# Attention and expert routing on one core: query transposes in a bank of their own, expert tiles transposed by TensorE, the last expert's weights loaded later

## The chip, the cores and the metric

The kernel runs on one core of one Trainium2 chip, as a single launch. The metric is the device time of one execution in microseconds. Three runs of the kernel before gave 455.08, 456.19 and 462.63 us.

## What is computed

An attention whose queries are averaged in pairs, and behind it a mixture of experts in which each token goes to one expert given with the input. Cut to what matters:

```python
# q, k, v: (8 batches, 8 heads, 1152, 64)
q_pool = q.reshape(B, H, S // 2, 2, D).mean(axis=3)          # 576 queries
scores = (1 / sqrt(D)) * q_pool @ k.transpose(0, 1, 3, 2)    # 576 x 1152
attn = exp(scores - max);  attn = attn / sum(attn)
x = (attn @ v) as (8 * 576 = 4608 tokens, 512)
for e in range(8):                                           # w1: 512 x 1024, w2: 1024 x 512
    mask = domain_id == e
    out[mask] = relu(x[mask] @ w1[e]) @ w2[e]
```

## The kernel before

**Attention.** Two heads of a batch make a pair; there are 32 pairs. The pooled queries and the keys of a pair are laid side by side (head, depth), so that the 128 partitions hold 64 depths of one head and 64 of the other. A pair has 12 steps (`SPP`), 384 in all. A step is `score` (L593, PE: scores of both heads, 432 columns each, into a tile `s` of two PSUM banks, three of which rotate), `expo` (L605, ACT: one `exp` over 128 x 864) and, some steps later, `av` (L614, PE: 15 small matmuls a call into the bank `acc`). `evac` (L626, L628, DVE) divides by the sums, `put_x` (L643) writes finished tokens to the DRAM tensor `x_tok`, from SyncE's queue.

**Transposing keys and queries.** `prep_q` (L531) adds the two queries of a pair of rows, `prep_k` (L546) copies keys. `turn(p)` (L565) transposes both on PE, in halves of 64 rows, as 2 x (9 + 6) = 30 transposes, into one of the three `s` tiles; DVE then takes the keys out as `kq` (L570) and the queries as `qz` in two strided copies (L575). It stands at the fifth step of each pair.

**Expert tiles inside attention.** A token list is built early (the `rt_*` and `id_*` functions). From step 112 on, `get_x` (L653, GpSimd) gathers 128 tokens of one expert as a tile `xs`. Each fill tile is then transposed, multiplied by w1 (`up`, L802, 32 matmuls) and by w2 (`down`, L815, 8 matmuls) in the one PSUM bank `px` (pool `xps`, one buffer), and scattered to the output (L515). Three of the tiles are transposed on PE (`turn_x`, L770), the others by a DMA transpose from SyncE's queue (`flip_x`, L668). A planner sets how much fill stands between the attention steps: it walks the steps, gives each kind of work a cost in ns (`C_T` a turn, 222 a fill piece) and issues pieces as long as the debt stays under `LAG`. The order that it writes is the order on each engine; a manual schedule keeps it.

```python
STEP, C_MODE, C_S, C_T, C_AV, LAG = 771, 200, 190, 440, 150, 250
...
            if debt + work_ns + c_ - span > LAG:
                break
            fb.piece()
```

No new tile begins in the last pair. What a begun tile still lacks at the end of attention is issued there in one go.

**Expert runs behind attention.** `runs` lists what is left: first expert 5 (tiles 0 to 2), then the rest of experts 0 to 4, then expert 5's last two tiles, then experts 6 and 7 whole (5 tiles each). A run k is `stage1` (L1042, 32 matmul groups) and `stage2` (L1075, 8 matmuls a tile). The tiles of run 1 and of runs with 5 tiles are transposed by PE (`turn_tile`, L1060); those of the short runs 2 to 6 by DMA (`flip_x`), which SyncE issues while run k - 1 goes on. Weights of experts 0 to 5 are loaded inside attention; those of 6 and 7 (`load_w`, L496 to L505, four parts of 512 KB each from GpSimd's queue) are put in a list `wq` behind a run, and each following run issues two parts from it:

```python
        if i1 == NTC and rest:
            er = rest.pop(0)
            fns, wts[er] = load_w(er)
            wq.extend(fns)
```

So 6 follows run 1 and 7 follows run 2; 7's parts are issued in runs 4 and 5.

Of the kernel before, what the change touches and what calls it, by code (L numbers as in the profile page):

```python
# [9 lines left out]
P = 128  # L10
# [9 lines left out]
def kernel(  # L20
# [537 lines left out]
    def turn(p):  # L558
        kp, qp = kpt[p], qpt[p]
        new_kq(p)  # L560
        mt = spsum.tile([P, 2, 512], FP32, name="s")[:, :, :].bitcast(F16)
        for c in range(NC + NJ):
            src = kp[:, c, :, :] if c < NC else qp[:, c - NC, :, :]
            for r, (lo, hi) in enumerate(HALF):
                nc.tensor.transpose(  # L565
                    mt[:, r, c * 64 : c * 64 + 64],
                    in_=src[lo:hi, :, :].rearrange("p h d -> p (h d)"),
                    identity=ident16[lo:hi, lo:hi],
                )
        nc.vector.tensor_copy(  # L570
            kq[p][:, :].rearrange("p (c r k) -> p r c k", c=NC, r=2),
            mt[:, :, 0 : NC * 64].rearrange("p r (c k) -> p r c k", c=NC),
        )
        for r, n in ((0, 64), (1, QP - 64)):
            nc.vector.tensor_copy(  # L575
                qz[p % 2][:, :].rearrange("p (j k) -> p j k", j=NJ)[:, :, 64 * r : 64 * r + n],
                mt[:, r, NC * 64 : (NC + NJ) * 64].rearrange("p (j k) -> p j k", j=NJ)[:, :, 0:n],
            )


# [107 lines left out]
    }  # L688
    STEP, C_MODE, C_S, C_T, C_AV, LAG = 771, 200, 190, 440, 150, 250
    FILL, HELD = 5, len(WSTEP)  # L690
# [70 lines left out]

    tiles, turned, begun, turns = [], [], [], []

# [11 lines left out]

    BY_PE = [(0, 0), (0, 1), (0, 2)]

    def add_tile(e, i):
        h0 = {"xs": (e, i)}
        tiles.append((e, i))  # L780

        def turn_pe():
            h0["xt"] = fill.tile([P, ND, P], F16, name="xt0")
            turn_x(h0["xt"][:, :, :], e, i)
            begun.append((e, i))

        def turn_in():
            h0["xt"] = fill.tile([P, ND, P], F16, name="xt0")
            flip_x(h0["xt"][:, :, :], e, i)
            h0["t"] = now[0]  # L790

        def up(f):
            if f == 0:
                h0["h"] = fill.tile([P, NF, P], F16, name="h0")
                if (e, i) not in BY_PE:
                    begun.append((e, i))
                    turned.append((e, i))
            if f % 4 == 0:
                h0["m"] = spare([P, 4, P])
            m = h0["m"]  # L800
            for cc in range(ND):
                nc.tensor.matmul(  # L802
                    m[:, f % 4, :], lhsT=wts[e][0][:, cc, f * P : (f + 1) * P],
                    rhs=h0["xt"][:, cc, :], start=cc == 0, stop=cc == ND - 1,
                )
            if f % 4 == 3:
                nc.vector.tensor_scalar(  # L807
                    out=h0["h"][:, f - 3 : f + 1, :], in0=m[:, :, :],
                    scalar1=0.0, scalar2=None, op0=ALU.max,
                )  # L810
# [15 lines left out]

        if (e, i) in BY_PE:
            fb.blocks.append(([turn_pe], 230, 1, False, h0))
        else:
            turns.append((e, i, turn_in, len(tiles) - 1))  # L830
        for fn, lo, hi in ((up, 0, 4), (up, 4, NF), (down, 0, NF)):
            fb.blocks.append(([lambda f=f, fn=fn: fn(f) for f in range(lo, hi)], 222, 1, (e, i) in BY_PE or lo > 0 or fn is down, h0))

# [58 lines left out]

    debt = 0
    for t in range(NST + 4):
# [12 lines left out]
        elif main and s_ in (2, 6) and p + 3 < NPAIR:  # L907
            (load_k if s_ == 2 else load_v)(p + 3)
        work_ns, span = 0, 0
        for it in windows.get(t, ()):  # L910
            if it < 0:
                turn(-it)
                work_ns += C_T
            else:
                score(it)
                expo(it)
                work_ns += C_S
                span += STEP
# [30 lines left out]

        if turns and t >= got.get(turns[0][:2], NST) + 10 and turns[0][3] <= len(begun):  # L950
            turns.pop(0)[2]()
        if first and t >= got.get(first[0], NST) + 8:
# [3 lines left out]
        while t == NST - SPP and fb.cur is not None:  # L956
            fb.piece()
        while main and span:
            if fb.cur is None:
                if not fb.blocks or t < fb.ready or t >= NST - SPP:  # L960
                    break
                b_ = fb.blocks[0]
                x_ = b_[4]["xs"]
                at = got.get(x_, NST) if x_ in BY_PE else b_[4].get("t", NST)
                if not b_[3] and t < max(at + 11, WSTEP[x_[0]][3] + 14):
                    break
                c_ = b_[1]
            else:
                c_ = fb.cur[1]
# [125 lines left out]
    for k_, r in enumerate(runs):  # L1095
# [22 lines left out]
        for fn in last:  # L1118
            fn()
        if i1 == NTC and rest:  # L1120
            er = rest.pop(0)
            fns, wts[er] = load_w(er)
            wq.extend(fns)
# [65 lines left out]
```

## Time and profile before

| | |
|---|---|
| median of 3 runs (lowest, highest) | 456.19 us (455.08, 462.63) |
| the profiled execution: its time, its span | 459.37 us, 457.1 us |
| instructions | 14379 |
| busy in the span: PE, PE weight load | 400.5 us (88%), 254.5 us (56%) |
| ACT, DVE, GpSimd | 339.4 us (74%), 222.4 us (49%), 182.2 us (40%) |
| mean of the granted TensorE clock | 0.958 |

The span is the time between the first and the last profiled instruction; the profiled execution's own time has 2.3 us outside of it. It is 3.2 us above the median. The shares are means over two stages with different limits: attention with fill (to about 333 us), and the expert runs (from there on).

### The profile page before, as it was taken

Reading aid. Unit: us, or ns where it says so; the run is one execution under the profiler, and the core shown is the slowest. Engines: PE = TensorE matmul, PEld = TensorE weight load, DVE = VectorE, ACT = ScalarE, POOL = GpSimd, SP = SyncE. Lnnn points to the kernel's source line nnn. Section 1 sums busy time; section 2 is a strip of 40 time slices with the busy share of each in tenths; the row PEclk is TensorE's granted clock in tenths of the full one; section 3 lists DMA queues with packets and bytes.
Section 4 is the critical chain, followed back from the end, with each engine's and each line's share of the span. In section 5 each row is a group of like instructions: output and inputs, shape, how many; then the busy total and the mean of one; then the engine's idle time right before and its main releaser. Section 6 shows DMA issues by size and latency. Waiting matters only on the chain.

```text
span 457.1 us, 14379 instructions
## 1 busy us (share of the span) xinstructions
PE 400.5 (88%) x6193; PEld 254.5 (56%) x6193; DVE 222.4 (49%) x612; ACT 339.4 (74%) x447; POOL 182.2 (40%) x304
## 2 busy tenths in 40 slices
PE   7888888888999987999999999989888989699993
PEld 4455555655666555566666665665545544365551
DVE  4388698864565443556655455634222322133230
ACT  5889999999999996999999999979822212133221
POOL 5433223307264240622642345534136686221413
PEclk9589999999999998999999999989889999799998
DMA  8999999976999999689999969956624499941203
GB/s 204 239 229 194 234 248 180 183 171 129 203 216 259 233 172 203 131 158 204 194 214 242 205 123 213 216 124 130 128 58 137 134 195 220 208 104 40 94 8 111
DMA packets 60107, 78.70 MB, mean 172 GB/s; under 512 B 19695, under 2 KB 48784, under 8 KB 60034
## 3 DMA queue, kind: packets, MB, share of 16 engines
q0 software_dynamic: 38384, 66.93, 72.6%
q1 hardware_dynamic: 21378, 10.63, 12.2%
q8 instruction: 50, 0.82, 0.7%
q14 instruction: 23, 0.19, 0.1%
q10 hardware_dynamic: 272, 0.13, 0.1%
HBM read 95.46 MB, written 15.21 MB: 242 GB/s over the span
## 4 chain that ended last, share of the span: by engine, by line
ACT 34%; PE 28%; issue 15%; DMA 8%; POOL 7%; DVE 4%; SPq 1%; POOLq 1%; another core or an unknown queue 1%; DVEq 0%; ACTq 0%
ACT e L605 34%; PE acc L614 9%; PE s L593 8%; PE px L802 4%; POOL out_dram L515 4%; DMA xt<-xs 3%; PE px L815 3%; POOL xs L653 2%; DMA w2h<-in_moe_w_dram 2%; DVE xb L628 2%; PE hp L1042 1%; PE s L565 1%; DMA q<-in_q_dram 1%; DMA x_tok<-xb 1%; SPq L643 1%
## 5 line engine op out<-in xcount | busy, mean ns | idle before, releaser
L605 ACT ACTIVATE e<-s 128x864 f16<-128x864 f32 x384 | 306.7, 948 | 18.0 <-PE s L593 16.5
L593 PE MATMUL s<-qz,kq 64*128 64x432 f16 (+2 forms) x1152 | 123.0, 294 | 24.1 <-ACT e L605 20.0
L614 PEld LDWEIGHTS <-e 128*128 128x128 f16 x2880 | 103.3, 99 | 47.2 <-issue 23.6
L614 PE MATMUL acc<-v,e 128*128 128x65 f16 x2835 | 122.8, 196 | 6.5 <-DVE xb L628 5.5
L653 POOL DMA_INDIRECT xs<-x_tok,grow x40 | 41.6, 1041 | 105.9 <-DVE xs L93 55.9
L593 PEld LDWEIGHTS <-kq 64*128 64x128 f16 x1152 | 46.8, 95 | 63.3 <-issue 46.2
L515 POOL DMA_INDIRECT out_dram<-osb,gid x40 | 40.9, 1022 | 76.2 <-ACT osb L1081 20.7
L1042 PE MATMUL hp<-xt,w1h 128*128 128x256 f16 (+3 forms) x320 | 45.9, 303 | 7.3 <-DMA xt<-xs 5.7
L1075 PE MATMUL op<-w2h,hT 128*128 128x512 f16 x216 | 49.5, 379 | 2.3 <-DVE hT L1049 1.3
L1047 ACT ACTIVATE hT<-hp 128x256 f16<-128x256 f32 (+2 forms) x36 | 17.7, 490 | 43.8 <-PE hp L1042 33.0
L114 POOL DMA_DIRECT2D vs<-in_v_dram x32 | 24.0, 749 | 60.3 <-DVE v L540 43.9
L1042 PEld LDWEIGHTS <-w1h 128*128 128x128 f16 x352 | 32.7, 100 | 26.8 <-issue 10.2
L1049 DVE TENSOR_SCALAR hT<-hp 128x256 f16<-128x256 f32 (+2 forms) x36 | 20.1, 558 | 51.4 <-PE hp L1042 35.3
L626 DVE RECIPROCAL rr<-acc 128x5 f32<-128x5 f32 x63 | 12.3, 195 | 66.0 <-PE acc L614 58.7
L1081 ACT COPY osb<-op 128x512 f32<-128x512 f32 x16 | 9.4, 585 | 42.3 <-PE op L1075 36.8
L570 DVE COPY kq<-s 128x1152 f16<-128x1152 f16 x31 | 23.4, 755 | 30.2 <-PE s L565 23.1
L802 PE MATMUL px<-xt,w1h 128*128 128x128 f16 x416 | 33.4, 224 | 4.2 <-DMA xt<-xs 2.9
L1075 PEld LDWEIGHTS <-hT 128*128 128x128 f16 x216 | 20.6, 98 | 25.7 <-DVE hT L1049 2.1
L628 DVE TENSOR_TENSOR xb<-acc,rr 128x320 f16<-128x320 f32 x63 | 31.0, 492 | 3.2 <-DMA x_tok<-xb 1.0
L815 PE MATMUL px<-w2h,h 128*128 128x512 f16 x104 | 31.6, 399 | 0.8 <-DVE h L807 0.8
L531 DVE TENSOR_TENSOR qp<-q 96x768 f16<-96x768 f32 x31 | 29.4, 947 | 2.3 <-DMA q<-in_q_dram 2.3
L802 PEld LDWEIGHTS <-w1h 128*128 128x128 f16 x416 | 24.7, 100 | 9.0 <-issue 7.5
(134 smaller groups left out, 301.3 us busy)
## 6 DMA issues: line engine op xcount, KB each, us to landing
q<-in_q_dram POOLq DMA_DIRECT2D x28, 576.0 KB
vs<-in_v_dram POOLq DMA_DIRECT2D x32, 288.0 KB
k<-in_k_dram POOLq DMA_DIRECT2D x31, 288.0 KB
w1h<-in_moe_w_dram POOLq DMA_DIRECT2D x16, 512.0 KB
w2h<-in_moe_w_dram POOLq DMA_DIRECT2D x16, 512.0 KB
x_tok<-xb SPq DMA_DIRECT2D x22, 96.0 KB
q<-in_q_dram SPq DMA_DIRECT2D x3, 576.0 KB
x_tok<-xb SPq DMA_DIRECT2D x22, 64.0 KB
```

Source lines behind the costliest of these rows:

```text
L114: nc.gpsimd.dma_start(vs[:, :, :, :], v[b, h : h + 2].rearrange("h (p c) d -> p h c d", p=P))
L515: ins = nc.gpsimd.indirect_dma_start(out=dst[:, :], out_offset=bass.IndirectOffsetOnAxis(ap=ap, axis=0), in_=src, in_offset=None, **kw,)
L531: nc.vector.tensor_tensor(out=qp[0:QP, :, :, :].rearrange("p j h d -> p h j d"), in0=q2[:, :, :, 0:D], in1=q2[:, :, :, D : 2 * D], op=ALU.add,
L593: nc.tensor.matmul(s[:, r, o : o + n], lhsT=kq[p][lo:hi, c * P : (c + 1) * P], rhs=qz[p % 2][lo:hi, q0 : q0 + n], start=True, stop=True,)
L605: nc.scalar.activation(e_[:, :, o : o + W], st.pop(t)[:, :, 0:W], AF.Exp, bias=0.0, scale=0.0625)
L614: nc.tensor.matmul(acc[p, h][:, i * (D + 1) : (i + 1) * (D + 1)], lhsT=et[p, c // 3][:, h, o : o + P], rhs=v16[p % NV][:, c, h, 0 : D + 1] ...
L628: nc.vector.tensor_tensor(out=xb[b][:, :, o : o + D], in0=a[:, :, 0:D], in1=rr[:, :].unsqueeze(2).broadcast_to([P, NQ, D]), op=ALU.mult,)
L653: nc.gpsimd.indirect_dma_start(out=dst, out_offset=None, in_=x_dram[0 : 1 + nb * Sp, :], in_offset=bass.IndirectOffsetOnAxis(ap=ap, axis=0),)
L802: nc.tensor.matmul(m[:, f % 4, :], lhsT=wts[e][0][:, cc, f * P : (f + 1) * P], rhs=h0["xt"][:, cc, :], start=cc == 0, stop=cc == ND - 1,)
L815: nc.tensor.matmul(h0["o"][:, :], lhsT=h0["h"][:, f, :], rhs=wts[e][1][:, f, :], start=f == 0, stop=f == NF - 1,)
L1042: nc.tensor.matmul(hp_[:, lo : lo + n], lhsT=w1h[:, cc, f * P : (f + 1) * P], rhs=xt[:, cc, lo : lo + n], start=cc == 0, stop=cc == ND - 1,)
L1075: nc.tensor.matmul(op_[:, :], lhsT=hT[:, f, i * P : (i + 1) * P], rhs=w2h[:, f, :], start=f == 0, stop=f == NF - 1,)
```

## The change

Four things change, all in the order and the place of work; what is computed stays.

1. `turn` transposes the keys alone. The queries of a pair get a function of their own, `turn_q`: 6 transposes over full 96 rows into the bank `px`, and one copy of 128 x 576 by DVE. It is issued one to five steps into the pair before, in a window in which no fill tile is open (pairs 0 and 1: at steps 10 and 7).
2. All fill tiles are transposed by PE (`turn_x`), 10 steps after their gather at the earliest. The list of DMA transposes in attention is gone. Those for expert 5's first run (`xf`) and those of the runs stay.
3. The planner's cost of a turn is 270 in place of 440, and a `turn_q` costs 300.
4. The weights of expert 7 are put in the list behind run 4 in place of run 2.

By the planner 11 fill tiles stand in attention where 13 stood: expert 0 has three, experts 1 to 4 have two each (before: three each for 0 to 2, two for 3 and 4). The runs 2 and 3 have three tiles each in place of two.

```diff
     def turn(p):
-        kp, qp = kpt[p], qpt[p]
+        kp = kpt[p]
         new_kq(p)
         mt = spsum.tile([P, 2, 512], FP32, name="s")[:, :, :].bitcast(F16)
-        for c in range(NC + NJ):
-            src = kp[:, c, :, :] if c < NC else qp[:, c - NC, :, :]
+        for c in range(NC):
             for r, (lo, hi) in enumerate(HALF):
                 nc.tensor.transpose(
                     mt[:, r, c * 64 : c * 64 + 64],
-                    in_=src[lo:hi, :, :].rearrange("p h d -> p (h d)"),
+                    in_=kp[lo:hi, c, :, :].rearrange("p h d -> p (h d)"),
                     identity=ident16[lo:hi, lo:hi],
                 )
...
-        for r, n in ((0, 64), (1, QP - 64)):
-            nc.vector.tensor_copy(
-                qz[p % 2][:, :].rearrange("p (j k) -> p j k", j=NJ)[:, :, 64 * r : 64 * r + n],
-                mt[:, r, NC * 64 : (NC + NJ) * 64].rearrange("p (j k) -> p j k", j=NJ)[:, :, 0:n],
-            )
+
+    def turn_q(p):
+        qt = xps.tile([P, Sp], F16, name="px")
+        for j in range(NJ):
+            nc.tensor.transpose(
+                qt[:, j * QP : (j + 1) * QP],
+                in_=qpt[p][0:QP, j, :, :].rearrange("p h d -> p (h d)"),
+                identity=ident16[0:QP, 0:QP],
+            )
+        nc.vector.tensor_copy(qz[p % 2][:, :], qt[:, :])
...
-    STEP, C_MODE, C_S, C_T, C_AV, LAG = 771, 200, 190, 440, 150, 250
+    STEP, C_MODE, C_S, C_T, C_AV, LAG = 771, 200, 190, 270, 150, 250
...
-        if (e, i) in BY_PE:
-            fb.blocks.append(([turn_pe], 230, 1, False, h0))
-        else:
-            turns.append((e, i, turn_in, len(tiles) - 1))
+        fb.blocks.append(([turn_pe], 230, 1, False, h0))
...
+        if span and p + 1 < NPAIR and s_ >= qat and qdone == p:
+            while s_ > 7 and fb.cur is not None:
+                fb.piece()
+                work_ns += 222
+            if fb.cur is None:
+                turn_q(p + 1)
+                fb.ready = t + 1
+                work_ns += C_Q
+                qdone += 1
...
-        if i1 == NTC and rest:
+        if k_ in (1, 4) and rest:
```

**What moves in the order.** DVE's order at the turn of a pair in attention (expert 1's first tile is the fill there; `L570`/`L569` takes the keys out, `L575`/`L582` the queries, `L807`/`L798` is the fill's relu). Before:

```order
L807 TENSOR_SCALAR h_2671<-px 128x512
L570 COPY kq<-s 128x2x9x64
L575 COPY qz_96<-s 128x6x64
L575 COPY qz_96<-s 128x6x32
L626 RECIPROCAL rr<-acc 128x5
```

After:

```order
L798 TENSOR_SCALAR h_2605<-px 128x512
L582 COPY qz_96<-px 128x576
L569 COPY kq<-s 128x2x9x64
L630 RECIPROCAL rr<-acc 128x5
L632 TENSOR_TENSOR xb<-acc,rr 128x5x64
```

The queries are one copy ahead of the keys' copy, out of `px` and no longer out of the `s` tile.

DVE's order at the end of attention, from the last pair's last evacuation to the first run's relu. Before:

```order
L626 RECIPROCAL rr<-px 128x5
L628 TENSOR_TENSOR xb<-px,rr 128x5x64
L807 TENSOR_SCALAR h_7626<-px 128x512
L821 COPY osb_7935<-px 128x512
L93 MEMSET xs 1x1 x2
L1049 TENSOR_SCALAR hT<-hp 128x384
```

After:

```order
L630 RECIPROCAL rr<-px 128x5
L632 TENSOR_TENSOR xb<-px,rr 128x5x64
L93 MEMSET xs 1x1 x2
L1044 TENSOR_SCALAR hT<-hp 128x384
L93 MEMSET xs 1x1
```

The rest of the thirteenth fill tile (the relu `h`, the copy `osb`, and on PE 16 and 8 matmuls ahead of them) no longer stands between attention and run 0.

GpSimd's order in run 4 and behind it (`L496`, `L499` are the first two parts of expert 7's weights, `L653`/`L657` the last two gathers, `L515` run results). Before:

```order
L653 DMA xs<-x_tok,grow 128x512
L496 DMA w1h<-in_moe_w_dram 128x2x1024
L652 MEMSET gap 1x1
...
L499 DMA w1h<-in_moe_w_dram 128x2x1024
L513 MEMSET gap 1x1
L515 DMA out_dram<-osb_8458,gid 4608x512
```

After:

```order
L657 DMA xs<-x_tok,grow 128x512
L513 MEMSET gap 1x1
L515 DMA out_dram<-osb_8230,gid 4608x512
...
L515 DMA out_dram<-osb_8260,gid 4608x512
L496 DMA w1h<-in_moe_w_dram 128x2x1024
L499 DMA w1h<-in_moe_w_dram 128x2x1024
```

Both parts move behind the three results of run 4, into run 5; the other two (`L502`, `L505`) move from run 5 to run 6.

## Rows read from the trace of the kernel before

**Rows 1.** The page's 40 slices of 11.4 us: ACT's busy tenths, granted TensorE clock

```profile
ACT  5889999999999996999999999979822212133221
...
PEclk9589999999999998999999999989889999799998
```

**Rows 2.** Groups by line: count, busy us, mean ns, idle before and its releasers

```profile
L605 ACT ACTIVATE e<-s 128x864 f16<-128x864 f32 x384 | 306.7, 948 | 18.0 <-PE s L593 16.5 <-PE px L802 0.7 <-PE acc L614 0.2
L802 PE MATMUL px<-xt,w1h 128*128 128x128 f16 x416 | 33.4, 224 | 4.2 <-DMA xt<-xs 2.9 <-DVE xb L628 1.3
L815 PE MATMUL px<-w2h,h 128*128 128x512 f16 x104 | 31.6, 399 | 0.8 <-DVE h L807 0.8
...
L725 DVE COPY qz<-s 64x576 f16<-64x576 f16 x1 | 0.4, 449 | 1.0 <-ACT qz L724 1.0
L720 PE MATMUL s<-ident,qp 96*128 96x96 f16 x6 | 0.4, 208 | 0.3 <-DVE qp L700 0.3
```

**Rows 3.** ACT in order of time: start, us, group [idle before, releaser]

```profile
120.83 2.52 ACT L605 ACTIVATE e<-s 128x864 f16<-128x864 f32 x3 [0.42 <-PE s L593]
...
177.48 1.67 ACT L605 ACTIVATE e<-s 128x864 f16<-128x864 f32 x2 [3.28 <-PE s L593]
```

**Rows 4.** PE in order of time around the turn in pair 11

```profile
119.99 0.43 PE L565 MATMUL s<-ident,kp 64*128 64x64 f16 x18
120.26 0.34 PE L565 MATMUL s<-ident,qp 64*128 64x64 f16 x12
120.44 0.35 PE L593 MATMUL s<-qz,kq 64*128 64x144 f16 x4
```

**Rows 5.** SyncE's issue, then PE, at the fourth fill tile (expert 3)

```profile
161.88 1.46 SPq L668 DMA_TRANSPOSE xt<-xs  x1
...
175.88 1.09 PE L802 MATMUL px<-xt,w1h 128*128 128x128 f16 x12 [2.93 <-DMA xt<-xs]
```

**Rows 6.** PE in pair 29's turn; windows: PE, PEld, DVE, ACT, POOL busy, clock, DMA, GB/s

```profile
303.37 0.25 PE L565 MATMUL s<-ident,qp 64*128 64x64 f16 x4 [0.47 <-issue]
...
302.00:306.00 4.00, 2.83 (x62) 1.85 (x60) 1.78 (x5) 2.43 (x4) 1.47 (x4) 1.00 0.68 144
306.00:309.40 3.40, 3.40 (x43) 2.75 (x40) 0.78 (x3) 2.42 (x4) 0.98 (x1) 0.50 0.18 59
```

**Rows 7.** PE in order of time, from the end of attention to run 5

```profile
333.15 0.31 PE L614 MATMUL px<-v,e 128*128 128x65 f16 x5
334.75 1.07 PE L802 MATMUL px<-xt,w1h 128*128 128x128 f16 x16 [1.29 <-DVE xb L628]
336.60 3.49 PE L815 MATMUL px<-w2h,h 128*128 128x512 f16 x8 [0.78 <-DVE h L807]
339.88 5.50 PE L1042 MATMUL hp<-xf,w1h 128*128 128x384 f16 x32
...
364.45 3.62 PE L1075 MATMUL op<-w2h,hT 128*128 128x512 f16 x16
367.90 3.66 PE L1042 MATMUL hp<-xt,w1h 128*128 128x256 f16 x32
...
377.90 5.36 PE L1042 MATMUL hp<-xt,w1h 128*128 128x384 f16 x32 [1.05 <-DMA xt<-xs]
383.10 5.34 PE L1075 MATMUL op<-w2h,hT 128*128 128x512 f16 x24
393.06 7.86 PE L1042 MATMUL hp<-xt,w1h 128*128 128x384 f16 x32 [4.62 <-DMA xt<-xs]
```

**Rows 8.** GpSimd's issues of expert 7's weights; windows around run 5 (columns as Rows 6)

```profile
381.30 0.80 POOL L496 DMA_DIRECT2D w1h<-in_moe_w_dram  x1
...
391.10 0.84 POOL L505 DMA_DIRECT2D w2h<-in_moe_w_dram  x1
...
378.00:388.40 10.40, 10.40 (x56) 5.29 (x54) 2.92 (x7) 2.55 (x5) 6.61 (x13) 1.00 1.20 221
393.10:398.20 5.10, 5.10 (x17) 2.33 (x18) 0.56 (x1) 0.98 (x2) 0.00 (x0) 0.50 1.44 212
```

More of the change, by code (lines that the diff above doesn't have):

```diff
@@ L760 @@
     fb = Fill()
-    tiles, turned, begun, turns = [], [], [], []
+    turned = []
     def spare(shape, dt=FP32):
@@ L774, in turn_x @@
         turned.append((e, i))
-    BY_PE = [(0, 0), (0, 1), (0, 2)]
     def add_tile(e, i):
         h0 = {"xs": (e, i)}
-        tiles.append((e, i))
         def turn_pe():
@@ L784, in turn_pe @@
             turn_x(h0["xt"][:, :, :], e, i)
[L785 to L790, printed above, removed]
         def up(f):
@@ L794, in up @@
                 h0["h"] = fill.tile([P, NF, P], F16, name="h0")
-                if (e, i) not in BY_PE:
-                    begun.append((e, i))
-                    turned.append((e, i))
             if f % 4 == 0:
@@ L825, in down @@
                 done[e] = i + 1
-        if (e, i) in BY_PE:
-            fb.blocks.append(([turn_pe], 230, 1, False, h0))
-        else:
-            turns.append((e, i, turn_in, len(tiles) - 1))
+        fb.blocks.append(([turn_pe], 230, 1, False, h0))
         for fn, lo, hi in ((up, 0, 4), (up, 4, NF), (down, 0, NF)):
-            fb.blocks.append(([lambda f=f, fn=fn: fn(f) for f in range(lo, hi)], 222, 1, (e, i) in BY_PE or lo > 0 or fn is down, h0))
+            fb.blocks.append(([lambda f=f, fn=fn: fn(f) for f in range(lo, hi)], 222, 1, True, h0))
     early = [(0, 0), (1, 0), (2, 0), (3, 0), (0, 1), (1, 1), (2, 1), (3, 1), (4, 0), (4, 1)]
@@ L891 @@
         windows[w[0] if w[0] >= 0 else w[1]] = w
-    debt = 0
+    debt, qdone, C_Q = 0, 0, 300
     for t in range(NST + 4):
@@ L909 @@
         work_ns, span = 0, 0
+        qat = 9 if p == 0 else 6 if p == 1 else 1
         for it in windows.get(t, ()):
@@ L948 @@
                 want.pop(0)
-        if turns and t >= got.get(turns[0][:2], NST) + 10 and turns[0][3] <= len(begun):
-            turns.pop(0)[2]()
         if first and t >= got.get(first[0], NST) + 8:
@@ L963 @@
                 x_ = b_[4]["xs"]
-                at = got.get(x_, NST) if x_ in BY_PE else b_[4].get("t", NST)
-                if not b_[3] and t < max(at + 11, WSTEP[x_[0]][3] + 14):
+                if not b_[3] and t < max(got.get(x_, NST) + 10, WSTEP[x_[0]][3] + 14):
                     break
```

## The prediction

> **What bounds the kernel now.** I read the page's slices first, because two stages with different limits follow each other. ACT is at 8 or 9 tenths up to slice 28 and falls to 2 behind it [rows 1]: attention up to about 333 us is paced by the exponentials, the expert runs behind it are not. Then the groups by line: in attention the 384 exponentials are busy for 306.7 us, and ACT stands idle for 18.0 us before them, 16.5 of these because the scores were not there [rows 2]. So attention can give back some 18 us at most, and only where PE is late with a score. Third, ACT and PE in order of time, to see where PE was late. One case is a wait for a DMA transpose: PE stood 2.93 us at the fourth fill tile, and ACT went empty for 3.28 us [rows 3, 5]. One is in pair 29, where PE had no instruction to run in the middle of a turn ("issue"), and the granted clock was 0.50 behind it; ACT lacked 4.00 - 2.43 = 1.57 us and 3.40 - 2.42 = 0.98 us in the two windows [rows 6]. The rest is spread over the start and the turns; in pair 11's turn ACT waited 0.42 us [rows 3]. Last, PE behind 333 us: the runs follow each other almost without a gap, except for what is left of the thirteenth fill tile, which stands between the last attention matmul and run 0, and for 4.62 us ahead of run 5, whose first stage then took 7.86 us where run 4's of the same size took 5.36 [rows 7]. So the tail is bound by PE, and by DMA at that one place.
>
> **The change, part by part.**
>
> *Query transposes.* In pair 11 the score behind the turn starts at 120.44, the query part at 120.26 and the whole turn at 119.99 [rows 4]; matmuls overlap, so by start times the queries hold PE for 0.18 us out of 0.45. That is what leaves the window in which scores are late. DVE loses one of two copies there, and the `s` tile comes free earlier, but I see no wait in these rows for that tile, so I count nothing for it. By the order, in every second pair from 22 to 30 (5 turns) `turn_q` stays in the same window behind the turn, and saves nothing; with the two first pairs aside, 24 turns shed 0.18 us. PE is late at about half of them as I read the trace, which gives 24 x 0.5 x 0.18 = 2.2 us. The bounds: nothing, and all idle time of ACT that the other two cases do not explain, 18.0 - 3.3 - 2.5 = 12.2 us.
>
> The new transposes themselves cost about what the trace shows for the same form at the start, 6 in 0.4 us and a copy of 576 columns in 0.45 us [rows 2]; they stand early in a pair, where the order has no fill piece. They share the one bank `px` with the fill. Of 104 matmuls of `down` and 416 of `up` PE waited for DVE to clear that bank once each, 0.8 and 1.3 us [rows 2], both of them at the very end of attention [rows 7]. In the new order a user of `px` follows directly on a `turn_q` at two places, both in the list building (steps 28 and 100); each waits at most for the copy of 0.45 us, so I take 0.5 us of loss of the 0.9.
>
> The Trainium skill ("Perfetto Trace Analysis", Optimizing Tensor Performance) advises the opposite of this sharing: independent groups should rotate through different PSUM banks, so that the evacuation of one overlaps the next. The trace agrees only so far that a bank with one buffer is safe while its users stand far apart. By the rule the sum would turn around; that is the last rival.
>
> *Fill tiles turned by PE.* The 3.28 us of ACT behind the DMA transpose go: it was issued at 161.88 and PE got its tile at 175.88, 14 us later [rows 5], while the gather ahead of it had landed before. With PE the tile needs the gather alone, and the order leaves 19 steps between the two for this tile, 13 at the least. What is late next is nothing that I can see, so 3.3 us. Ten more DMA transposes leave SyncE's queue, which also carries the writes to `x_tok`; they were hidden, and I count nothing. Eight more transposes on PE (four matmuls and a copy each) are paid for in the planner's budget, as are the dearer turns (270 + 300 against 440): not by time but by fill, 11 tiles in place of 13.
>
> *Pair 29.* Whether instructions run late again there cannot be read from an order. The loss was 1.57 + 0.98 = 2.5 us [rows 6]; between nothing and all of it I take half, 1.3.
>
> *The end of attention.* Before, the last attention matmul ended at 333.15 + 0.31 = 333.46, and run 0 began at 339.88 [rows 7], 6.4 us later. In the new order nothing stands between them. Run 0 still needs a score bank to be read out; I take 0.5 us for it, and 5.9 us gained. The cover of this: the gathers of run 1 start when `x_tok` is written, and were hidden behind the left-over tile and run 0.
>
> *Two more tiles behind attention.* A third tile in a run costs 5.36 - 3.66 = 1.70 us in the first stage and 5.34 - 3.62 = 1.72 us in the second [rows 7], both at full clock. Two of them are 6.8 us lost. Their transposes go by DMA during the run before, their scatters through GpSimd, both beside PE.
>
> *Expert 7's weights.* In 378 to 388.4 us the DMA engines are full (1.20) and the parts go out from 381.30 to 391.10 [rows 8], while the three transposes for run 5 are under way. Run 5 lost 4.62 us of waiting, and 7.86 - 5.36 = 2.50 us because the clock was 0.50 after the gap [rows 7, 8]. Moved by a run, the first part stands behind run 4's results, and the transposes for run 5 have only expert 6's parts beside them. The transposes for run 6, two in place of three, are issued when run 4's first stage ends, one second stage (5.34 us [rows 7]) ahead of these parts. So I count all 7.1 us as gained, and nothing as the lower bound. The parts have run 6's rest and all of run 7 to land.
>
> **The sum.** Attention: 2.2 - 0.5 + 3.3 + 1.3 = 6.3 us. Tail: 5.9 - 6.8 + 7.1 = 6.2 us. Together 12.5 us off the profiled execution's 459.4 us, or 446.9 us (2.3 us of it outside the span, which stay). That execution is 3.2 us above the median of 456.19, and no term depends on what made it so; from the median the time is 443.7 us.
>
> **The rivals.**
>
> - *The stall moves to run 6.* The transposes for run 6 meet expert 7's parts as those for run 5 did. For it: the parts still go out within a run of them, and the DMA engines were full for long. Against it: they are fewer, and issued earlier. The 7.1 us stay: 450.8 us.
> - *The gain at the end of attention is given back ahead of run 1.* Its two tiles can be gathered only when the last tokens are written; if run 0 ends before they are there, PE waits for up to the 5.9 us by which it came earlier: 449.6 us. Against it: run 0 alone takes over 10 us (5.50 in its first stage, and a second of 5.34 by run 4's [rows 7]).
> - *All waits of the turns go.* If the lateness comes from the length of the turn as a whole, from the `s` tile held by three copies, the 12.2 us come in place of 2.2: 433.7 us. Against it: the startup's share of the idle time is in these 12.2 too.
> - *The bank `px` becomes the bound, and the kernel slower.* Each of 31 `turn_q` waits for the fill's evacuation (0.78 us at the end of attention [rows 7]) and the next fill for the copy (0.45 us [rows 2]), PE works strictly in order, and the scores queue behind it. All of it would cost 31 x 1.23 = 38 us: 481.8 us. From 12.5 / 31 = 0.4 us a turn on the gain is gone. Against it: the order keeps a window between them at 29 of 31 places.
>
> **How the numbers follow.** 0.55 for the sum as worked out, with a range of its own of 437 to 449 us; 0.18 for the stall that moves, 0.10 for the gain given back, 0.10 for all waits gone, 0.05 for the bank, 0.02 for what I don't see. The range of 434 to 452 us leaves out the bank, the better half of "all waits gone", and the cases in which one of the first two rivals meets a poor attention stage, about 0.18. Two per cent of 456.19 us is 9.1 us, about what a measurement of this kernel can tell from no change; faster by more is a time under 447.1 us. Nine in ten of the main case, all of "all waits gone" and a fifth of the first two rivals lie there, 0.65; the rest of these within two per cent, 0.28; slower 0.07.
>
> **What the profile after would show.** Right: no idle time of PE for a DMA-made `xt` in attention; ACT's idle time before the exponentials some 6 us smaller than 18.0; the first matmul of run 0 within 1 us of the last attention matmul; runs 2 and 3 longer by 3.4 us each; no wait of several us ahead of run 5 or 6, and no stretch of half clock there. Wrong: idle time of PE or ACT put down to the copy of `qz` out of `px`; a wait ahead of run 1; a new wait for a transpose ahead of run 6. The prediction fails most easily in the two terms of which I took a part by judgement (the turns, pair 29), and in that all 7.1 us of run 5 hang on one cause.

## The result and the profile after

| | before | after |
|---|---|---|
| median of 12 runs (lowest, highest) | 456.71 us (455.01, 462.92) | 451.81 us (448.95, 454.67) |
| ratio, 95% interval | | 0.9891 [0.9854, 0.9927] |
| the profiled execution: time, span | 459.37, 457.1 us | 454.67, 452.9 us |

The kernel got 4.9 us faster (3.3 to 6.7 by the interval), not 12.5. The time lies 0.2 us inside the range, at its end.

The kernels of one section below ran on one chip. By the kernel before, the sections are of two kinds: in some its median is 455 to 457 us, as here, in others 447 to 448; they are called the 456 us and the 447 us sections. Whether the chip makes the difference is not settled: the record gives the chips of the five sections below the numbers 3, 8, 10, 2 and again 3, so that number 3 stands for a section of either kind. Ratios leave out executions over 1.5% slower than the fastest of the same kernel, so that they can differ a little from the quotient of the medians.

Attention came out near the forecast in sum. The page's slices and the groups by line of the kernel after, beside [rows 1, 2]:

```profile
ACT  4989999999999989999999999979821222233321
...
PEclk9699999999999999999999999989997999899997
```

```profile
L609 ACT ACTIVATE e<-s 128x864 f16<-128x864 f32 x384 | 305.6, 963 | 11.7 <-PE s L597 9.3 <-PE acc L618 1.4
...
L793 PE MATMUL px<-xt,w1h 128*128 128x128 f16 x352 | 27.7, 223 | 0.0
L806 PE MATMUL px<-w2h,h 128*128 128x512 f16 x88 | 25.0, 380 | 0.0
L582 DVE COPY qz<-px 128x576 f16<-128x576 f16 x31 | 14.0, 453 | 4.9 <-PE px L577 4.7 <-issue 0.2
```

ACT's idle time fell from 18.0 to 11.7 us, `up` (L793) and `down` (L806) wait for nothing any more, and the last attention matmul ends at 326.30 in place of 333.46 us. Of the rest the largest piece is pair 29 again. ACT in order of time, beside [rows 6]:

```profile
299.36 2.46 ACT L609 ACTIVATE e<-s 128x864 f16<-128x864 f32 x3 [1.83 <-PE s L597]
302.24 1.67 ACT L609 ACTIVATE e<-s 128x864 f16<-128x864 f32 x2 [0.42 <-PE s L597]
304.80 5.94 ACT L609 ACTIVATE e<-s 128x864 f16<-128x864 f32 x7 [0.89 <-PE s L597]
```

The tail did not. PE in order of time from run 0 to run 6, beside [rows 7]:

```profile
326.81 3.50 PE L1037 MATMUL hp<-xf,w1h 128*128 128x384 f16 x20 [0.51 <-PE px L618]
330.88 2.11 PE L1037 MATMUL hp<-xf,w1h 128*128 128x384 f16 x12 [0.58 <-ACT hT L1042]
332.83 5.34 PE L1070 MATMUL op<-w2h,hT 128*128 128x512 f16 x24
338.01 0.39 PE L1055 MATMUL hp<-ident,xs 128*128 128x128 f16 x4
338.92 0.40 PE L1055 MATMUL hp<-ident,xs 128*128 128x128 f16 x4 [0.52 <-DMA xs<-x_tok,grow]
339.84 1.92 PE L1037 MATMUL hp<-xt,w1h 128*128 128x256 f16 x16 [0.52 <-issue]
343.42 0.60 PE L1037 MATMUL hp<-xt,w1h 128*128 128x256 f16 x4 [1.66 <-DVE xs L93]
346.92 2.72 PE L1037 MATMUL hp<-xt,w1h 128*128 128x256 f16 x12 [2.90 <-ACT hT L1042]
349.43 4.81 PE L1070 MATMUL op<-w2h,hT 128*128 128x512 f16 x16
354.07 5.36 PE L1037 MATMUL hp<-xt,w1h 128*128 128x384 f16 x32
...
375.84 5.36 PE L1037 MATMUL hp<-xt,w1h 128*128 128x384 f16 x32 [0.84 <-DMA xt<-xs]
381.04 5.34 PE L1070 MATMUL op<-w2h,hT 128*128 128x512 f16 x24
388.65 7.04 PE L1037 MATMUL hp<-xt,w1h 128*128 128x384 f16 x32 [2.27 <-DMA xt<-xs]
...
400.71 3.66 PE L1037 MATMUL hp<-xt,w1h 128*128 128x256 f16 x32
```

Run 0 (L1037 out of `xf`) starts 0.51 us behind attention, as forecast. But run 1 (from 339.84) stands still twice, 1.66 and 2.90 us, and its second stage takes 4.81 us, at a mean granted clock of 0.74 (349.4 to 354.0 us), where one of the same size took 3.62 before (364.45 in [rows 7]). Run 5 (388.65) still waits 2.27 us and then takes 7.04 in place of 5.36. Run 6 waits for nothing.

The profile does not name what run 1 waits for ("remote" is a releaser that it does not know); by the order of the program it is PE itself. ACT in order of time, in run 1:

```profile
340.54 0.38 ACT L1042 ACTIVATE hT<-hp 128x256 f16<-128x256 f32 x1 [1.26 <-issue]
346.48 0.38 ACT L1042 ACTIVATE hT<-hp 128x256 f16<-128x256 f32 x1 [5.56 <-remote]
```

The relu at 346.48 waits for the third of the four groups that PE began from 339.84 on, all of them done by 341.76 if one goes by their starts. PE's ends are modelled. I read the row as a completion that reached ACT some 5 us later than the starts say, and call such completions late; no run shows it directly. The next matmuls need the bank that the relu empties.

Expert 7's first part goes out as run 5 starts now (L496 at 388.29, run 5 at 388.65; GpSimd in order of time, L505 is the last part of expert 6), while the DMA engines are as full ahead of run 5 as before; beside [rows 8], with the same columns:

```profile
372.75 0.80 POOL L505 DMA_DIRECT2D w2h<-in_moe_w_dram  x1 [1.48 <-DMA w1h<-in_moe_w_dram]
388.29 0.81 POOL L496 DMA_DIRECT2D w1h<-in_moe_w_dram  x1
```

```profile
361.30:371.30 10.00, 10.00 (x56) 5.29 (x55) 2.93 (x8) 3.03 (x6) 7.55 (x14) 1.00 1.19 138
371.30:381.30 10.00, 9.16 (x52) 4.78 (x50) 2.43 (x7) 3.13 (x6) 5.27 (x11) 1.00 1.27 193
```

The tail as a ledger, in us behind the end of the last attention matmul. The last four rows are from traces of 447 us sections, told of below.

| trace | attention ends at | run 0 | run 2 | run 4 | run 5 | run 6 | end of span |
|---|---|---|---|---|---|---|---|
| before | 333.46 | 6.4 | 27.1 | 44.4 | 59.6 | 72.5 | 123.6 |
| after | 326.30 | 0.5 | 27.8 | 49.5 | 62.4 | 74.4 | 126.6 |
| before (f2) | 329.77 | 4.9 | 23.5 | 40.9 | 53.9 | 64.3 | 115.5 |
| after (f1) | 317.62 | 0.5 | 20.4 | 44.2 | 57.8 | 68.2 | 119.6 |
| after (i0) | 317.25 | 0.5 | 20.0 | 41.4 | 58.8 | 70.6 | 121.9 |
| weights spread (i1) | 318.63 | 0.5 | 20.0 | 40.7 | 51.1 | 61.5 | 114.2 |

### The profile page after: what moved, and what is told of

Read it like the earlier page. It is cut to its first block, busy times and chain, and to the rows that moved or that the text cites. A ratio compares the mean times of both kernels' runs of the same rounds, so it can differ in the third digit from the quotient of the medians.

```text
span 452.9 us, 13900 instructions
## 1 busy us (share of the span) xinstructions
PE 401.3 (89%) x5975; PEld 253.4 (56%) x5975; DVE 222.7 (49%) x583; ACT 340.4 (75%) x449; POOL 184.5 (41%) x304
## 5 line engine op out<-in xcount | busy, mean ns | idle before, releaser
L609 ACT ACTIVATE e<-s 128x864 f16<-128x864 f32 x384 | 305.6, 963 | 11.7 <-PE s L597 9.3
L618 PEld LDWEIGHTS <-e 128*128 128x128 f16 x2880 | 101.5, 98 | 42.5 <-issue 23.8
L657 POOL DMA_INDIRECT xs<-x_tok,grow x40 | 41.9, 1048 | 102.4 <-DVE xs L93 37.1
L515 POOL DMA_INDIRECT out_dram<-osb,gid x40 | 42.2, 1055 | 73.2 <-ACT osb L1076 32.1
L1037 PE MATMUL hp<-xt,w1h 128*128 128x384 f16 (+3 forms) x320 | 49.7, 316 | 8.2 <-DMA xt<-xs 3.1
L1070 PE MATMUL op<-w2h,hT 128*128 128x512 f16 x232 | 53.5, 385 | 0.0
L1037 PEld LDWEIGHTS <-w1h 128*128 128x128 f16 x352 | 32.6, 101 | 31.9 <-issue 12.9
L1042 ACT ACTIVATE hT<-hp 128x384 f16<-128x384 f32 (+2 forms) x36 | 18.5, 514 | 39.7 <-PE hp L1037 32.3
L1044 DVE TENSOR_SCALAR hT<-hp 128x384 f16<-128x384 f32 (+2 forms) x36 | 21.1, 587 | 53.5 <-PE hp L1037 38.8
L1070 PEld LDWEIGHTS <-hT 128*128 128x128 f16 x232 | 22.7, 99 | 25.8 <-issue 1.6
L569 DVE COPY kq<-s 128x1152 f16<-128x1152 f16 x31 | 23.4, 756 | 21.3 <-PE s L564 16.0
L793 PE MATMUL px<-xt,w1h 128*128 128x128 f16 x352 | 27.7, 223 | 0.0
L806 PE MATMUL px<-w2h,h 128*128 128x512 f16 x88 | 25.0, 380 | 0.0
L123 POOL DMA_DIRECT2D k<-in_k_dram x31 | 23.2, 750 | 3.9 <-DVE vs L93 2.4
```

What stands on the lines that cost most here:

```text
L515: ins = nc.gpsimd.indirect_dma_start(out=dst[:, :], out_offset=bass.IndirectOffsetOnAxis(ap=ap, axis=0), in_=src, in_offset=None, **kw,)
L609: nc.scalar.activation(e_[:, :, o : o + W], st.pop(t)[:, :, 0:W], AF.Exp, bias=0.0, scale=0.0625)
L618: nc.tensor.matmul(acc[p, h][:, i * (D + 1) : (i + 1) * (D + 1)], lhsT=et[p, c // 3][:, h, o : o + P], rhs=v16[p % NV][:, c, h, 0 : D + 1] ...
L657: nc.gpsimd.indirect_dma_start(out=dst, out_offset=None, in_=x_dram[0 : 1 + nb * Sp, :], in_offset=bass.IndirectOffsetOnAxis(ap=ap, axis=0),)
L793: nc.tensor.matmul(m[:, f % 4, :], lhsT=wts[e][0][:, cc, f * P : (f + 1) * P], rhs=h0["xt"][:, cc, :], start=cc == 0, stop=cc == ND - 1,)
L806: nc.tensor.matmul(h0["o"][:, :], lhsT=h0["h"][:, f, :], rhs=wts[e][1][:, f, :], start=f == 0, stop=f == NF - 1,)
```

## The experiments

Theory of the forecast: each edit is worth its term. The rival, from the trace after: run 2 can't begin before some 27 us behind attention whatever run 0 does, and runs 4 and 5 wait because the DMA engines are full as a whole, not because of expert 7's parts.

**One edit at a time (a 456 us section; before 456.31 us).** The weights put back in the changed kernel (e1), the weights alone in the kernel before (e2), the fill tiles alone in the kernel before (e3), one tile more as fill in the changed kernel (e4):

```diff
e1 -        if k_ in (1, 4) and rest:
e1 +        if i1 == NTC and rest:
e2 -        if i1 == NTC and rest:
e2 +        if k_ in (1, 4) and rest:
e3 -    BY_PE = [(0, 0), (0, 1), (0, 2)]
e3 +    BY_PE = [(e, i) for e in range(FILL) for i in range(NTC)]
e4 -    STEP, C_MODE, C_S, C_T, C_AV, LAG = 771, 200, 190, 270, 150, 250
e4 +    STEP, C_MODE, C_S, C_T, C_AV, LAG = 771, 200, 190, 240, 150, 250
e4 -    debt, qdone, C_Q = 0, 0, 300
e4 +    debt, qdone, C_Q = 0, 0, 200
```

> The changed kernel with only the place of expert 7's weights put back (behind run 2, so their parts go out in runs 4 and 5). If these parts made the stall ahead of run 5, as the forecast had it, the wait of 4.62 us and the slow first stage of run 5 (7.86 us) come back and the kernel is 7.1 us slower than the changed one, about 459 us. If the DMA engines are full there mainly from expert 6's weights and the gathers, as the trace of the changed kernel suggests (it still waits 2.27 us there), the edit is worth what the two traces differ by, 7.1 - 3.95 = 3.1 us, about 455 us.

Measured: 451.79 us, 0.985 [0.981, 0.989]. That is no loss against the changed kernel's 0.989. Its one trace has the old stall in full (5.07 us ahead of run 5, 7.89 for the stage), but that execution took 456.41 us, 4.6 above its median. No base ran beside it.

> The kernel before with only expert 7's weights moved behind run 4. By the forecast 7.1 us faster than before (about 449.6 us) and no wait ahead of run 5. By the reading of the trace after, 3 us faster (about 453.7 us), with some 2 us of wait left ahead of run 5. A third way: runs 2 and 3 are a tile shorter here than in the changed kernel, so expert 6's parts go out faster, the DMA engines are as full as ever when run 5's transposes are due, and the gain is under 1.5 us.

Measured: 454.34 us, 0.9977 [0.9939, 1.0014]: 1.0 us faster, between 2.8 faster and 0.6 slower. The third way comes closest. PE in order of time, runs 4 and 5:

```profile
379.46 5.36 PE L1042 MATMUL hp<-xt,w1h 128*128 128x384 f16 x32 [2.53 <-DMA xt<-xs]
384.65 5.34 PE L1075 MATMUL op<-w2h,hT 128*128 128x512 f16 x24
389.83 5.36 PE L1042 MATMUL hp<-xt,w1h 128*128 128x384 f16 x32
```

Run 5 (389.83) waits for nothing, and run 4 waits 2.53 us in place of 1.05: part of the stall moved forward.

> The kernel before with all fill tiles transposed by PE and nothing else; by its planner 12 tiles, one less than before, and none left over at the end of attention. By the terms of the forecast: 3.3 us for the flip's wait, 5.9 us for the earlier start of run 0, less 3.4 us for one more tile behind attention: 5.8 us faster than before, about 451 us. If the earlier start of run 0 is given back ahead of run 1, as in the trace of the changed kernel, 3.3 - 3.4 = 0: no change, with idle time of PE in run 1's first stage of 4 us or more.

Measured: 452.88 us, 0.9942 [0.9902, 0.9981]: 2.6 us faster, between the two. ACT's idle time is 11.8 us in place of 18.0, as small as in the changed kernel (11.7) without its query part, and attention ends at 326.59, 6.9 us earlier:

```profile
L605 ACT ACTIVATE e<-s 128x864 f16<-128x864 f32 x384 | 306.0, 946 | 11.8 <-PE s L593 10.6 <-PE acc L614 0.6
```

Run 0 starts 3.0 us behind attention, run 2 27.65 us behind it: its earlier start was given back here too.

> The changed kernel with lower planner costs (turn 240 for 270, query turn 200 for 300), which put one tile more into attention (12 in place of 11; run 2 has two tiles in place of three). By the forecast's term for a tile 3.4 us faster than the changed kernel, about 448.4 us, with attention as long as before. If the planner's costs are what keeps PE ahead of the exponentials, attention gets longer by about what the tile costs on PE (41 pieces' share, up to 3.4 us) and the time stays at about 452 us.

Measured: 448.44 us, 0.9852 [0.9803, 0.9901]. Attention ends at 326.46, the left-over tile stands ahead of run 0 (which starts 6.7 us behind attention), and run 2 still begins 27.4 us behind it. So in this trace the tile costs nothing there, and a run is a tile shorter.

**Executions, transposes, tokens (a 447 us section; before 447.36 us).** f1 is the changed kernel, f2 the kernel before. f3 has PE transpose run 2's tiles, f4 fills four tiles from older lists:

```diff
f3 -                if 0 < k_ and j1 - j0 < NTC:
f3 +                if 1 < k_ and j1 - j0 < NTC:
f4 +        c = i - 3 if e < 2 and i > 2 else i
f4 -        nb = [ib // NQ for k_, ib in zip(KO[1:], IB) if (i + 1) * P <= k_] + [B]
f4 +        nb = [ib // NQ for k_, ib in zip(KO[1:], IB) if (c + 1) * P <= k_] + [B]
f4 -        gather(x_[:, :], grow[:, e * NTC + i : e * NTC + i + 1], nb[0])
f4 +        gather(x_[:, :], grow[:, e * NTC + c : e * NTC + c + 1], nb[0])
```

> The changed kernel once more, to see which of its idle times come back. Attention should end near 326 us in the trace again. If the late matmul completions in run 1 (some 6 us) and the wait ahead of run 5 (2.27 us, and a slow stage behind it) belong to the program, both are within 1 us of the first trace; if they differ from one execution to the next, one of them is off by 2 us or more, and by about as much the time is off its median of 451.8 us.

> The kernel before once more, for one look. The prediction took 7.1 us at run 5 from one trace, of an execution 3.2 us above the median. If the stall belongs to the program, the wait ahead of run 5 is 4 to 5 us again and the stage behind it about 7.9 us; if it differs between executions, it is smaller here, by 2 us or more, and the time lies nearer to 456 us or below.

Measured: the kernel before 447.64 us in its one run, the changed kernel 439.07 us, 0.9845 [0.9772, 0.9918], so 6.9 us faster than before by the ratio (3.7 to 10.2 by the interval). The exponentials in f2 and then in f1:

```profile
L605 ACT ACTIVATE e<-s 128x864 f16<-128x864 f32 x384 | 305.4, 954 | 15.6 <-PE s L593 15.3
```

```profile
L609 ACT ACTIVATE e<-s 128x864 f16<-128x864 f32 x384 | 304.0, 983 | 4.8 <-PE s L597 3.5 <-PE acc L618 0.5
```

PE of f1 in runs 1, 2, 4 and 5:

```profile
331.03 3.67 PE L1037 MATMUL hp<-xt,w1h 128*128 128x256 f16 x32 [0.52 <-DVE xt L1059]
334.54 3.62 PE L1070 MATMUL op<-w2h,hT 128*128 128x512 f16 x16
337.99 5.36 PE L1037 MATMUL hp<-xt,w1h 128*128 128x384 f16 x32
...
361.83 6.81 PE L1037 MATMUL hp<-xt,w1h 128*128 128x384 f16 x32 [2.91 <-DMA xt<-xs]
...
375.42 5.36 PE L1037 MATMUL hp<-xt,w1h 128*128 128x384 f16 x32 [1.61 <-DMA xt<-xs]
```

Run 1 has no late completions here, so they are no property of the program alone. In attention ACT's idle time falls by 10.8 us from f2 to f1, and attention ends 12.2 us earlier. In f2 runs 4 and 5 wait 3.32 and 2.48 us, 5.8 together; in f1 it is 2.91 + (6.81 - 5.36) + 1.61 = 6.0 us. Expert 7's weights were moved, and the stall stayed.

> The changed kernel with run 2's three tiles transposed by PE between run 1's results, so that no DMA transpose is under way during run 1. They cost PE about 3 x 0.4 = 1.2 us. In all six traces so far run 2 begins 27.1 to 27.8 us after the last attention matmul, however early run 0 began. If the DMA transposes hold run 1 back, its late completions go and run 2 begins at about 0.5 + 18.3 + 1.2 = 20 us: 6 to 7 us faster than the changed kernel, about 445 us. If they have nothing to do with it, run 2 begins at 28 to 29 us, and the time is the same or 1 us worse.

Measured: 433.80 us, 0.9750 [0.9688, 0.9813], 5.3 us faster than f1, but not for the reason given: run 2 begins 20.4 us behind attention in f1 and 20.5 in f3. What is gone is every wait ahead of runs 4 and 5.

> The changed kernel with other tokens in four gathers: the last two tiles of experts 0 and 1 are filled from the lists of their first two tiles, which lie in batches written long before, so that the gathers need not wait for the last x_tok (other rows reach these tiles). If the write of x_tok holds run 1 back (the rival of the prediction), the gathers go out some 3.5 us earlier, and run 2 begins as much earlier: about 448 us. If the gathers' time does not matter, run 2 begins at 27 to 28 us as before, with the same late completions in run 1, and the time stays at about 452 us.

Measured: 435.68 us. The gathers start 3.4 us earlier, run 1 only 0.4 (13.0 for 13.4 us behind attention). So the write of `x_tok` hardly holds run 1 here, where run 1 isn't late in the first place. The 3.4 us gained lie at runs 4 and 5 again, which wait for nothing.

**Parts again (a 447 us section; before 448.08 us).** g0 is f3; g1 is f3 with e1's edit; g2 is f3 with e4's; g3 is the changed kernel with parts 2 and 4 undone.

> The kernel with run 2's tiles transposed by PE once more, as the base for the two behind it and to see its gain on another chip: 0.975 of the kernel before was measured, 5 us faster than the changed kernel on the same chip. If the late completions of PE in run 1 are caused by run 2's DMA transposes, they are missing here even on a chip that shows them in the changed kernel, and run 2 begins some 20.5 us after the last attention matmul; if not, run 2 begins at 25 us or later here on such a chip, and the gain is smaller.

Measured: 436.20 us, 0.9818 [0.9726, 0.9909]; one wait of 2.2 us ahead of run 5, where the same kernel had none in f3's trace. Run 2 begins 20.5 us behind attention; as run 1 isn't late in this section with any kernel, the question on the late completions stays open here.

> Run 2's tiles by PE, and expert 7's weights back behind run 2. If the place of these weights is what makes the stall ahead of run 5 (the forecast), the wait and the slow stage come back, up to 7.1 us. If the stall is the DMA engines' whole load, with transposes of 2-byte elements as the part that tipped it, nothing comes back: runs 4 and 5 follow without a wait of over 1 us, within 1 us of the base.

Measured: 436.50 us, 0.3 more than its base. In the one trace run 5 loses 4.6 us in place of 2.2; over six runs the place of the weights makes no difference.

> Run 2's tiles by PE, and one tile more as fill (planner costs 240 and 200 in place of 270 and 300; its turn lies in attention, its 24 matmul steps behind it, ahead of run 0). The left-over costs about 6.5 us of PE time behind attention, a tile in run 2 less gives 3.4 us. If run 1 has nothing else to wait for, the time is 3 us worse than the base; if run 1 has a wait of 6 us for other reasons, the left-over fills it and the time is 3.4 us better.

Measured: 445.52 us, 0.9968 [0.9881, 1.0055], by the ratios 6.7 us more than its base; its fastest execution (439.62) is behind the slowest of the base (436.78). In the trace, of an execution 3.6 us above its median, attention ends at 323.29 in place of 318.63 us, and run 2 begins 28.3 us behind it in place of 20.5. Where run 1 isn't late, a tile kept in attention costs more than it saves.

> The changed kernel without its second and fourth part: the queries are transposed by themselves and the planner's costs are the new ones, but the fill tiles after the third come by DMA transpose as before, and expert 7's weights stand behind run 2. By the forecast's terms: 2.2 us for the turns less 0.5 for the shared bank, and half of pair 29's 2.5; the flip's wait (3.3) stays, so attention is 3 us shorter than before and ACT idle some 15 us of 18. By the trace of the kernel with the second part alone, where ACT's idle time fell to 11.8 us without the query part, the flips are worth 6 us and the query part about nothing: attention as long as before but for the one tile less.

Measured: 443.38 us; the ratio of 0.989 [0.966, 1.012] settles nothing. In the trace ACT's idle time is 10.8 us (15.6 in f2, 4.8 in f1):

```profile
L609 ACT ACTIVATE e<-s 128x864 f16<-128x864 f32 x384 | 304.7, 972 | 10.8 <-PE s L597 9.4 <-PE acc L618 0.5
```

By these three traces, from two sections, the query part and the new planner costs are worth 4.8 us of idle time, and the fill tiles by PE 6.0. Of the 4.8 us, 2.2 lie at the first fill tile that a DMA transposes, and not at the turns: ACT stands there for 2.35 us in g3 and for 4.58 in f2 (ACT in order of time):

```profile
177.07 1.67 ACT L605 ACTIVATE e<-s 128x864 f16<-128x864 f32 x2 [4.58 <-PE s L593]
```

**What fills the DMA engines (a 456 us section; before 455.47 us).** h0 is the changed kernel, h1 has PE transpose the tiles of all runs, h2 is f3, h3 leaves expert 6's loads out:

```diff
h1 -                if 0 < k_ and j1 - j0 < NTC:
h1 +                if j1 - j0 > NTC:
h3 +            if er == 6:
h3 +                wts[er] = wts[4]
h3 +            else:
...
```

> The changed kernel as the base of the three behind it on the same chip: some 8 us faster than before where the matmuls of run 1 complete in time, some 5 us where they are late; waits ahead of runs 4 and 5 of 4 to 7 us together with the slow stage behind them.

Measured: 449.99 us, 0.9877 [0.9833, 0.9922]; run 1 is late again, run 2 begins at 26.0, and runs 4 and 5 wait 0.76 and 3.12 us.

> The changed kernel with the tiles of all runs transposed by PE, so that no DMA transpose is left behind attention but those of run 0. By the trace three tiles cost run 1's second stage 0.45 us, so 14 tiles cost some 2.1 us. If it is the transposes that are late (their own queue, behind full DMA engines), no run waits any more, and the kernel is 4 to 6 us faster than the base, within 1 us of the one with run 2's tiles alone. If the gathers ahead of them are late too, the waits move to the transposes on PE (for xs), and half or more of the waits stay.

Measured: 450.11 us, the same as its base. No run waits for a transpose, but three tiles cost 0.67 us a run (11.05 in place of 10.38), and the late completions are there with no DMA transpose near. PE in order of time, run 1:

```profile
341.64 0.60 PE L1037 MATMUL hp<-xt,w1h 128*128 128x256 f16 x4 [0.85 <-issue]
344.43 1.01 PE L1037 MATMUL hp<-xt,w1h 128*128 128x256 f16 x4 [2.19 <-issue]
```

> Only run 2's tiles by PE, on the same chip as the base: 5 us faster than it by the first pair of runs. If run 1's completions are late in the base on this chip and they come from run 2's DMA transposes, they are gone here.

Measured: 451.12 us, no gain in this section. Run 1 is late, and the waits ahead of runs 4 and 5 stay at 0.62 and 2.65 us. f3's gain was not safe.

> The changed kernel without the loads of expert 6's weights (run 7 uses expert 4's). If runs 4 and 5 wait because expert 6's 2 MB fill the DMA engines while their transposes are due, the waits go and the kernel is 4 to 6 us faster than the base. If the transposes are slow by themselves or wait for gathers, the waits stay, within 1 us.

Measured: 447.44 us, 2.6 less than its base, under the 4 to 6 expected, and single executions overlap (444.62 to 448.96 against 445.63 to 452.82). In the trace runs 4 and 5 wait for nothing, and the tail is 118.6 us in place of 123.7. Two windows, 35 to 55 us behind attention as those of the changed kernel above, columns as in [rows 6]:

```profile
359.80:369.80 10.00, 10.00 (x56) 5.33 (x55) 2.71 (x8) 3.13 (x6) 5.98 (x12) 1.00 0.52 140
369.80:379.80 10.00, 10.00 (x56) 5.34 (x55) 2.93 (x7) 3.13 (x6) 4.94 (x11) 1.00 0.45 131
```

Expert 6's 2 MB are what fills them: 0.45 to 0.52 busy without, 1.19 to 1.27 with them in the first trace after.

**The version that follows (a 447 us section; before 446.99 us).** i0 is the changed kernel, i1 sends expert 6's parts one a run:

```diff
i1 -        h = stage1(wts[e][0], xt[k_], n * P, {**at, 2: part, 7: part})
i1 +        h = stage1(wts[e][0], xt[k_], n * P, {**at, **({2: part} if k_ > 5 else {}), 7: part})
```

> The changed kernel as the base of the next one on the same chip: waits ahead of runs 4 and 5 of 3 to 7 us together with a slow stage behind them if there is one.

> The changed kernel with expert 6's weights sent one part of 512 KB a run (runs 2 to 5) in place of two (runs 2 and 3); expert 7's go two a run in runs 6 and 7. If the whole load of the DMA engines between the gathers and these 2 MB makes runs 4 and 5 wait, half of the load there is gone and the waits with it: 3 to 5 us off the tail in the trace, 2 to 4 us faster than the base, toward the kernel without these loads (2.6 us faster than its base). If any single part of 512 KB beside a run's transposes makes it wait, the waits spread over runs 3 to 6 and the time stays. New wait that could come: run 7 or 8 for the last parts.

Measured: i0 439.20 us, 0.9799 [0.9745, 0.9853]; i1 433.16 us, 0.9666 [0.9617, 0.9715]. By the medians i1 is 6.0 us faster than the changed kernel (its slowest execution, 434.65, is ahead of the base's fastest, 437.42) and 13.8 faster than before, the best of all runs. The edit also moves expert 7's parts a run further back; in i0 they go out from 376.02 us on, as run 5 starts, so they can't be what it waits for. PE at run 5, i0 and then i1:

```profile
376.01 6.84 PE L1037 MATMUL hp<-xt,w1h 128*128 128x384 f16 x32 [6.82 <-DMA xt<-xs]
```

```profile
364.56 5.34 PE L1070 MATMUL op<-w2h,hT 128*128 128x512 f16 x24
369.74 5.36 PE L1037 MATMUL hp<-xt,w1h 128*128 128x384 f16 x32
```

In i1's trace no run waits. The line on the transposes (L672) in i0 and then in i1, from issue to landing:

```profile
DMA to landing us min/median/max: 2.9/10.0/20.2
```

```profile
DMA to landing us min/median/max: 2.8/5.8/11.1
```

By stretch, those issued from 317 to 340 us, ahead of expert 6's parts, land after 2.9 to 4.9 us in i0 and 2.8 to 4.9 in i1; those issued from 350 to 360 us, among these parts, after 15.1 to 20.2 and 5.8 to 8.2.

## Why the prediction was wrong

*Attention* (forecast 6.3 us, measured 7.2 in the first pair of traces, 12.2 in a 447 us section). Right in sum, by other pieces; that the sum came so near is in part luck. The flip's wait went. In the 456 us sections e3, which has the fill tiles by PE and no query part, already has ACT's idle time down by 6.2 us, and the whole change by 6.3: the fill tiles show more than the 3.3 us that I took, and the query part nothing of its 2.2 (e3 has one fill tile fewer than before and one more than the changed kernel). In the 447 us sections g3 against f2 leaves 4.8 - 2.2 = 2.6 us for the turns, near my 2.2. Pair 29 came back in the first trace after, and not in f1. `px` cost about the 0.5 us that I took: PE waited 0.6 us at one place of the list building (L461, for the copy of `qz`), and L793 and L806 idle 0.0. The Trainium skill ("Perfetto Trace Analysis", Optimizing Tensor Performance) would have independent groups rotate through several PSUM banks; one bank was enough here, because its users stand apart in the order.

*The earlier start of run 0* (5.9 us). The start came as forecast; the step that failed is that nothing behind it would wait. In the 456 us sections run 2 begins 25.8 to 27.8 us behind attention in all ten traces, with run 0 at 0.4 or at 6.7. From 6.4 and 27.1 before it went to 0.5 and 27.8: 6.6 us lost between run 0 and run 2, more than was gained. That is the rival "given back ahead of run 1" in place and size, but not by its mechanism: the gathers were there (0.52 us of waiting). In the 447 us sections 3.1 of 4.4 us were kept. The trace of before had a sign of it, which I passed over as "almost without a gap": PE in run 1, first and second stage, before:

```profile
352.53 3.65 PE L1042 MATMUL hp<-xt,w1h 128*128 128x256 f16 x32 [1.53 <-ACT xt L1066]
...
358.58 2.12 PE L1075 MATMUL op<-w2h,hT 128*128 128x512 f16 x9 [0.89 <-DVE hT L1049]
```

*Two more tiles* (6.8 us lost). Right: runs 2 and 3 take 5.36 and 5.34 us a stage, 3.4 us more each.

*Expert 7's weights* (7.1 us). This is the step that failed everywhere. I read a wait for run 5's transposes beside expert 7's parts as a wait caused by these parts, and counted "all 7.1 us as gained". Waits and slow stages of runs 4 and 5 together went from 1.05 + 4.62 + 2.50 = 8.2 to 0.84 + 2.27 + 1.68 = 4.8 us in the first pair of traces, and from 5.8 to 6.0 in a 447 us section. By itself the edit gave 1.0 us (e2), and undone it cost 0.3 (g1). The cause is expert 6's four parts, sent two a run beside these transposes: without them the waits are gone (h3), and at half their density too (i1). They do it together with the rest that is queued: with the parts as they were, the waits also went in f3 and f4 (not in h2, and in g0 but for 2.2 us), and in h1, where the runs need no DMA transpose. The stall also differs between executions. In four traces of the changed kernel it is 4.8, 3.9, 6.0 and 8.8 us, and the execution from which I took 7.1 us was 3.2 above the median.

The sum in the first pair of traces: attention -7.2; tail -5.9 + 6.6 + 6.8 - 3.4, less 2.2 us of small waits in runs 2 and 3 that before had, and 1.0 us more at the very end: +2.9. Together -4.3 us of span, where -12.5 was forecast. What did not come are the 6.6 us between run 0 and run 2 and 3.7 of the 7.1 us at runs 4 and 5.

The rival of the stall at run 6 did not come (400.71, no wait), nor did that of the bank. "All waits of the turns go" came near in the 447 us sections, where ACT's idle time fell to 4.8 us in f1 and to 4.5 in i0.

Open: why run 1 is held in the 456 us sections, and whether it is PE's completions that are late, as I read them. It happens without DMA transposes near (h1) and without expert 6's loads (h3), and a smaller loss is there with a late run 0 too (e4: 1.74 us ahead of run 1's first stage, 0.83 in its second). The gathers and the scatters of run 0 that run beside run 1 were not taken away in such a section.

## What to carry to other kernels

For a transfer that lands late, look at all that was queued in the time it took, up to 20 us here, and not at what is issued while the engine waits; spreading the bulk load beside it was worth 6 us where moving the load behind it was worth about one. A stall in one trace is one sample: set that execution beside the median, and look at a second trace, before a term takes all of it. An earlier start counts only up to the next place at which the work behind it is held by something else.

## What was not expected of the hardware

- The same kernel differs by 2% from section to section: the medians of the kernel before were 455.5 to 456.7 us in some and 447.0 to 448.1 in others. It is not shown that the chip makes it (number 3 ran in both kinds). In the former ACT got the results of run 1's matmuls up to 5 us after their recorded starts, with a granted clock of 1.00 when that began (0.50 from 346 us on).
- Full DMA engines are not fast ones: 1.19 busy at 138 GB/s with expert 6's loads (361.3 to 371.3 us after), 0.52 busy at 140 GB/s without them (h3). The Trainium skill ("DMA: Bandwidth & Descriptors", Rules for kernel authors) says that DMAs of SyncE, ScalarE and GpSimd run on the same 16 DMA engines and interleave. The traces agree: transposes from SyncE's queue landed up to 20.2 us after their issue beside GpSimd's weight loads at two parts a run (i0), and up to 11.1 at one (i1).
